# Reordering the second chunk's attention work on ScalarE, VectorE and TensorE in a fused mLSTM and GELU kernel

## The chip, the cores and the metric

The kernel runs on one core of a Trainium2 chip. The metric is the time of one execution on the device in microseconds (us); several runs are taken and their median is compared. The engines are called as the profile has them: PE is TensorE (PEld its weight loads), DVE is VectorE, ACT is ScalarE, POOL is GpSimd, SP is SyncE, which issues most DMA transfers. Each engine works through its own instructions in order and waits on semaphores for the others.

## What is computed

The reference has two parts. The first is an mLSTM cell over q, k, v of shape (4 batches, 8 heads, 768 steps, 40 dimensions), with gates i, f and o:

```
m_new  = max(f + m, i)
f_stab = exp(f + m - m_new);  i_stab = exp(i - m_new)
C = f_stab * C + i_stab * outer(v, k);   n = f_stab * n + i_stab * k
y = sigmoid(o) * (C @ q) / max(|n . q|, 1)
```

The second takes the 3072 rows of y as x (3072 x 320) and computes `g = h * sigmoid(1.702 h)` with `h = x @ w_in` (320 x 2048), and then `g @ w_out` (2048 x 320).

## The kernel before

The 768 steps are cut into six chunks of 128 (w = 0 to 5). Inside a chunk the cell is computed in matrix form: scores of keys against queries times a matrix of decay weights, then products with v; from chunk to chunk a state (40 x 41 for each of 32 head pairs, two heads above each other on the partitions) is carried. From w = 1 on a chunk is worked in two halves of 64 steps, with `state_mid` between them. Work is further cut into two groups of 16 heads, c = 0 and 1.

The main loop goes over the chunks. For each w TensorE first does the up products of that chunk (x times w_in, `up` for w = 0, `up_fast` from w = 1 on), and then the down products (`down` or `down_fast`) in small blocks. Between the blocks of chunk w the attention work of chunk w + 1 is interleaved: `attention(w)` returns a dictionary from a block's number to the calls that are made right after that block. So for w = 0 there are 16 blocks of `down` (L835, eight recorded matmuls of 128x320 each), in the order batch 0, 1, 2, 3 with two blocks each for the first half of w_out, then the same for the second half; among them stands the attention work of the second chunk, w = 1. That stage runs from 65.9 to 108.6 us in the profile, and the change lies in it.

The order of every engine's instructions is that of the program text (a manual schedule); semaphores follow from what each instruction reads and writes. The names that matter, with their lines in the kernel before:

- `fill_squares(q_sq)` (L119, ACT): two copies that complete the square layout of the queries, which two DMA transfers have brought. `block_transposes` (L415, DVE) then turns them into qT, four times 128x512.
- `columns` (L387, L391, ACT): exponentials of per-step factors, kept in `cols`.
- `weights_exp(1, c)` (L463, ACT): 16 exponentials of 128x64. `weights_mask(1, c)` (L470, POOL): two masks over 64 partitions each.
- `scale` (L619, POOL) makes vw, `decay` (L610) multiplies a state by its decay factor; on POOL for state_mid, on DVE inside `carry`.
- `carry(1, c)`: products of keys and vw on TensorE (L633), and additions of the result to the decayed states on DVE (L642). The decay of the second half (L610 on DVE) stands between the two additions.
- `convert(n)`: one piece (128x512) of the expert weights, from 64-bit words to floats: two ACT instructions (L254, L258, `convert_begin`) and four DVE instructions (L270, L275, L281, L282, `convert_end`). Pieces 17, 18 and 19 are the last ones of w_out.
- `weight_sums` (L847, POOL): differences of quarters of w_out, kept in t_sb. `keep_w01` (L914, issued on POOL): a copy of one quarter to DRAM.
- `scores(1, c)`: products on TensorE (L490) and a multiplication with the masked weights on DVE (L493). `values(1, c)`: products with v (L534) and with the states (L542), then DVE forms y: L548 and L549 add them, L500 to L509 divide and gate.
- PSUM holds eight banks: four are taken by the four open sums of `down`, and two pairs (`banks`) go round among carry, scores and values: scores take the pairs that carry wrote, the values of a group take both pairs, one for L534 and one for L542.
- `seam_out`, `seam_in`, `seam_turn`: y goes to DRAM and back in square blocks (for c = 0 issued on SP, for c = 1 on ACT; the way back on SP), and DVE turns it (L603). `split_x` (ACT, L765) and `split_on` (DVE, L773 and on) cut x into a high and a low part for the up products of chunk 1.
- `split_high`, `split_rest` (ACT), `split_diff`, `split_low`, `split_rest_low` (DVE): the same for w_in.

The calls of `attention(1)` are listed in `calls`, and `at` gives for each entry the block behind which it is made. Before the change scores stand behind block 6 (counted from 0), the two values behind 8 and 9.

Of the kernel before, what the change touches and what calls it, by code (L numbers as in the profile page):

```python
# [14 lines left out]
OP = mybir.AluOpType  # L15
# [17 lines left out]
def kernel(  # L33
# [81 lines left out]
    def fill_squares(t):  # L115

        x = t[:, 32:].rearrange("r (m d) -> r m d", d=D)
        for i in (0, 64):
            A.copy(out=x[i + 32:i + 64, :, 0:D - 32], in_=x[i:i + 32, :, 32:D])  # L119
# [124 lines left out]
    def convert(n):  # L244
        convert_begin(n)
        convert_end(n)

    def convert_begin(n):
        convert_high(n)
        convert_low(n)  # L250
# [9 lines left out]
    def convert_end(n):  # L260
        convert_mid(n)
        convert_add(n)
# [116 lines left out]
    def columns(w):  # L379
        if w == 0:  # L380
            pt = banks("p_cols")[:, 0, :]
            T.transpose(pt[:, 0:3 * BH], stacked[w], full)
            c = cols[w] = gate.tile([L, 4 * BH], FP, bufs=1, name="cols")
            A.activation(out=c[:, 2 * BH:3 * BH], in_=pt[:, 2 * BH:3 * BH], func=AF.Exp, scale=-1.0)
            return
        c = cols[w]
        A.activation(out=c[:, BH:3 * BH], in_=c[:, BH:3 * BH], func=AF.Exp, scale=-1.0)  # L387
        d = raw[w][:, 3 * BH:].rearrange("p (j i x) -> p i x j", i=2, x=2)
        for i in range(2):
            r = slice(i * 64, i * 64 + 64)  # L390
            A.activation(out=c[r, 3 * BH:].rearrange("p (x j) -> p x j", x=2), in_=d[r, i], func=AF.Exp)  # L391
# [233 lines left out]
    def carry(w, c):  # L625
        js = slice(c * NJ, (c + 1) * NJ)
        pc = banks("p_c")
        n = 2 if 0 < w < NW - 1 else 1
        for j in range(NJ):
            for i in range(2):  # L630
                for x in range(n):
                    t = slot(i, x) if w else slice(0, L)
                    T.matmul(pc[i * 64:i * 64 + D, x, j * D1:(j + 1) * D1], k_cols(w, t, c * PH + 2 * j + i),  # L633
                             vw[w, c][t, 2 * j + i, :], start=True, stop=True)
        new = lambda x: pc[:, x, 0:NJ * D1].rearrange("r (j d) -> r j d", d=D1)
        if w == 0:
            A.copy(out=state[1][:, js], in_=new(0))
            return
        for x, dst in enumerate((state_mid, state[1 - w % 2])[:n]):
            if x:  # L640
                decay(w, c, x, V)
            V.tensor_tensor(out=dst[:, js], in0=new(x), in1=dst[:, js], op=OP.add)  # L642


    def up(w, j, between, first=None):

# [72 lines left out]
    def split_diff(n):  # L719
        V.scalar_tensor_tensor(out=w_diff[1, n], in0=w_high[n], scalar=-1.0 - 1.0 / BASE, in1=w_in[n], op0=OP.mult,  # L720
                               op1=OP.add)

    def split_low(n, engine):
        if n < 2:
            w_low[n] = win.tile([128, 2, 512], FR, tag="wa" if n else "wb", name="w_low")
        engine.tensor_tensor(out=w_low[n] if n < 2 else w_low[1, n], in0=w_in[n], in1=w_high[n], op=OP.subtract)
# [17 lines left out]
    def split_rest_low():  # L744
        wr = w_rest[0]
        V.tensor_tensor(out=wr[64:128, 0::2], in0=w_in_x[0:64], in1=wr[0:64, 0::2], op=OP.subtract)
        V.tensor_tensor(out=wr[64:128, 1::2], in0=w_in_x[64:128], in1=wr[64:128, 1::2], op=OP.subtract)
# [164 lines left out]
    def keep_w01():  # L912
        w01_row.append(rows.tile([128, NH, DH], FP, tag="w01", bufs=1, name="w01_row"))
        G.dma_start(out=w01_row[0], in_=w01)  # L914
# [112 lines left out]
    fetched = {0: range(10, 13), 1: range(13, 18), 3: (18, 19)}  # L1027

    def attention(w):
        at = (0, 1, 3, 3, 5, 6, 8, 8, 9, 11, 12, 13) if w == 1 else (0, 0, 1, 3, 2, 4, 5, 6, 6, 10, 11, 11)  # L1030
        calls = [[(columns, w)][w == 1:] + [(scale, w, 0), (scale, w, 1), (decay, w, 0, 0), (decay, w, 1, 0)],
                 [(weights_mask if w == 1 else weights, w, 0)], [(weights, w, 1)], [(carry, w, 0), (carry, w, 1)], [(open_gates, w)],
                 [(scores, w, 0), (scores, w, 1)], [(values, w, 0)], [(seam_out, w, 0), (seam_in, w, 0)],
                 [(values, w, 1), (seam_out, w, 1), (seam_in, w, 1)], [(seam_turn, w, 0), (split_x, w, 0)], [(seam_turn, w, 1), (split_x, w, 1)], [(split_on, w)]]
        if w == 1:
            calls[2:4] = [], calls[3] + [(weight_sums, 0)] + calls[2]
        side = {}
        for i, c in zip(at, calls):
            side.setdefault(i, []).extend(c)
        return side  # L1040

    for w in range(NW):
# [119 lines left out]
        for i, block in enumerate(blocks):  # L1162
            if w == 0 and i == 0:
                columns(1)
                convert_begin(17)
                weights_exp(1, 0)
                fill_squares(q_sq)
                convert_end(17)
                for n in (1, 3, 5, 7):
                    block_transposes(1, n)  # L1170
            if w == 0 and i in (4, 5):
                convert(14 + i)
            if w + 2 < NW and i == (6 if w == 0 else 0):
                load_gates(w + 2)
            if w == 0 and i == 13:
                load_squares(w + 2, "k")
            if w == 0 and i == 15:
                load_squares(w + 2, "q")
            block()
            run(side.get(i, []))  # L1180
            if w == 1 and i == 4:
                last_sums(1, 0, (2, 3))
            if w == 0 and i == 5:
                keep_w01()
                wait_for(w_out_flat[1][:, 4 * 512:])
                weight_sums(1)
                weight_sums(3)
            if w == 0 and i == 5:
                split_high(0)
                split_rest()  # L1190
                split_high(1)
            if w == 0 and i == 9:
                split_diff(0)
                split_low(0, V)
                split_rest_low()
            if w and more:
                if i == 11:
                    fetch_diff(w + 1, (0, 1))
                    fetch_low(w + 1)
                    if w + 2 < NW:  # L1200
                        load_squares(w + 2, "k")
                if w + 2 == NW and i == 8:
                    room_out(0, 8, 8, "k_sq", 2592)
                    out_part(0, 8)
                    out_part(0, 12)
                if i == 13:
                    fetch_diff(w + 1, (2, 3))
                    if w + 2 == NW:
                        fetch_w01()
                    if w + 2 < NW:  # L1210
                        load_squares(w + 2, "q")
# [30 lines left out]
```

## Time and profile before

| | us |
|---|---|
| median of 3 runs | 443.29 |
| lowest and highest | 443.14, 443.64 |
| the profiled execution | 444.92 |
| its span, first to last instruction | 443.2 |
| stage with the change, first down product to first fast up product | 65.9 to 108.6 |
| TensorE busy over the span | 438.0 |
| VectorE, ScalarE, GpSimd busy | 349.5, 246.2, 130.4 |

The granted TensorE clock of the run was 1.0. The chain of waits is followed back from the last instruction: at each step to what released it, or to the instruction before it on the same engine. In a timeline a row gives the start and the duration in us, the engine, the line, the operation, what it writes and reads with shapes, and, in brackets, how long the engine was idle before it and what ended that. "x4" means that four like instructions are merged into one row.

### The profile page before, as it was taken

How to read it: one execution, taken by the hardware profiler on the slowest of the kernel's cores; microseconds unless marked ns; L12 is line 12 of the kernel's file. 1: busy time of each engine (PE TensorE's matmuls, PEld its weight loads, DVE VectorE, ACT ScalarE, POOL GpSimd, SP SyncE). 2: the span in 40 equal slices, each digit the busy share in tenths (PEclk: the TensorE clock that was granted, in tenths of full speed). 3: DMA queues.
4: the chain of work that ended last, by engine and by line, in shares of the span. 5: the costliest groups of instructions: out<-in, count | busy, mean ns of one | idle time of the engine just before them, and what ended most of it. 6: DMA issues, size and time to landing. Idle time of an engine off the chain costs nothing.

```text
span 443.2 us, 12203 instructions
## 1 busy us (share of the span) xinstructions
PE 438.0 (99%) x4967; PEld 382.1 (86%) x4967; DVE 349.5 (79%) x701; ACT 246.2 (56%) x536; POOL 130.4 (29%) x133
## 2 busy tenths in 40 slices
PE   8999999999999999999999999999999999999996
PEld 6877887777889999888999888999888999988996
DVE  4898998989999876779686778686769656988990
ACT  5676779902887701687701486900386912397720
POOL 6411337540066700135700044710035620022100
PEclk9999999999999999999999999999999999999999
DMA  8999999227779327979226997305999305810000
GB/s 168 195 291 224 239 246 186 61 47 191 179 204 175 48 66 218 236 101 190 34 54 167 288 112 164 58 19 139 308 154 159 61 19 137 276 61 0 3 29 30
DMA packets 130008, 61.37 MB, mean 138 GB/s; under 512 B 102128, under 2 KB 122592, under 8 KB 129952
## 3 DMA queue, kind: packets, MB, share of 16 engines
q1 hardware_dynamic: 120512, 54.86, 57.7%
q10 hardware_dynamic: 8768, 4.28, 3.3%
q0 software_dynamic: 672, 1.46, 1.3%
q8 instruction: 39, 0.64, 0.7%
q14 instruction: 17, 0.14, 0.1%
HBM read 49.76 MB, written 10.81 MB: 137 GB/s over the span
## 4 chain that ended last, share of the span: by engine, by line
PE 97%; DVE 1%; DMA 1%; issue 0%; ACT 0%; SPq 0%; DVEq 0%
PE p_out L888 28%; PE p L806 17%; PE p_h L806 17%; PE p_out L835 8%; PE p_h L657 7%; PE p L963 6%; PE p L534 2%; PE p L490 2%; PE p L542 2%; PE p L633 2%; PE p_h L666 2%; PE p L406 2%; PE p_s L479 1%; PE p_o L524 1%; DMA k_sq<-in_k_dram 1%; DVE state L610 0%
## 5 line engine op out<-in xcount | busy, mean ns | idle before, releaser
L856 POOL TENSOR_TENSOR g<-g 128x512 f32<-128x512 f32 x16 | 20.6, 1298 | 119.4 <-ACT g L784 119.4
L888 PE MATMUL p_out<-w_out,g 128*128 128x160 f32 x384 | 55.2, 300 | 0.0
L888 PEld LDWEIGHTS p_out<-w_out,g 128*128 128x128 f32 x384 | 53.1, 190 | 0.5
L765 ACT ACTIVATE x_high<-xT 128x512 fp32r<-128x512 f32 x10 | 6.3, 632 | 76.9 <-DVE xT L603 76.9
L784 ACT ACTIVATE g<-g 128x512 f32<-128x512 f32 x80 | 46.4, 628 | 2.9 <-DVE g L825 2.7
L823 ACT ACTIVATE g<-p 128x512 f32<-128x512 f32 x40 | 21.8, 597 | 34.9 <-PE p L806 33.5
L825 DVE SCALAR_TENSOR_TENSOR g<-p,g 128x512 f32<-128x512 f32 x40 | 25.7, 684 | 18.5 <-ACT g L823 10.5
L463 ACT ACTIVATE wt<-wt,cols 128x64 f32<-128x64 f32 x160 | 39.0, 341 | 0.1
L888 PE MATMUL p_out<-t_sb,s 128*128 128x160 f32 x256 | 37.8, 301 | 0.0
L893 DVE TENSOR_TENSOR o_sb<-o_sb,p_out 128x160 f32<-128x160 f32 x56 | 16.8, 319 | 26.4 <-PE p_out L888 26.2
L888 PEld LDWEIGHTS p_out<-t_sb,s 128*128 128x128 f32 x256 | 35.5, 190 | 0.2
L835 PE MATMUL p_out<-w_out,g 128*128 128x320 f32 x128 | 35.7, 436 | 0.0
L835 PEld LDWEIGHTS p_out<-w_out,g 128*128 128x128 f32 x128 | 23.9, 190 | 9.6
L825 DVE SCALAR_TENSOR_TENSOR g<-p_h,g 128x512 f32<-128x512 f32 x40 | 25.9, 680 | 5.6 <-PE p_h L806 5.0
L657 PE MATMUL p_h<-xT,w_in 128*128 128x256 f32 x128 | 29.8, 385 | 0.1
L657 PEld LDWEIGHTS p_h<-xT,w_in 128*128 128x128 f32 x128 | 23.6, 190 | 5.4 <-issue 2.2
L823 ACT ACTIVATE g<-p_h 128x512 f32<-128x512 f32 x40 | 23.3, 597 | 7.9 <-PE p_h L806 7.9
L470 POOL TENSOR_SCALAR_AFFINE_SELECT wt<-wt 64x1024 f32<-64x1024 f32 x20 | 24.3, 1217 | 7.1 <-ACT wt L463 6.2
L806 PE MATMUL p_h<-x_diff,w_diff 128*128 128x512 f32 x80 | 25.1, 394 | 0.0
L806 PE MATMUL p<-x_rest,w_rest 128*128 128x512 f32 x80 | 25.1, 395 | 0.0
L806 PE MATMUL p_h<-x_rest,w_rest 128*128 128x512 f32 x80 | 25.0, 394 | 0.0
L806 PE MATMUL p<-x_diff,w_diff 128*128 128x512 f32 x80 | 25.0, 393 | 0.0
(224 smaller groups left out, 1051.6 us busy)
## 6 DMA issues: line engine op xcount, KB each, us to landing
w_diff<-w_row SPq DMA_DIRECT2D x16, 512.0 KB, 5.7
wt<-m_row SPq DMA_DIRECT2D x20, 256.0 KB, 5.3
bits<-in_moe_w_in_dram SPq DMA_DIRECT2D x8, 512.0 KB, 8.4
out_dram<-o_sb SPq DMA_DIRECT2D x24, 160.0 KB, 3.0
q_sq<-in_q_dram SPq DMA_DIRECT2D x10, 320.0 KB, 9.1
eo<-in_o_gate_dram SPq DMA_DIRECT2D x5, 640.0 KB, 6.6
bits<-in_moe_w_out_dram SPq DMA_DIRECT2D x8, 320.0 KB, 5.6
q_sq<-x_row SPq DMA_DIRECT2D x10, 256.0 KB, 2.7
```

What stands on the lines that cost most here:

```text
L463: A.activation(out=x[:, h, :], in_=x[:, h, :], func=AF.Exp, scale=-1.0, bias=cols[w][:, c * PH + h:c * PH + h + 1])
L470: G.affine_select(out=r, in_=r, compare_op=OP.is_ge, fill=0.0, base=0, pattern=[[0, PH], [1, HL]], channel_multiplier=-1)
L657: T.matmul(ph[j][i][:, t], w_in[f // 4][:, c, f % 4 * 128:f % 4 * 128 + 128], x[:, c, t], start=(first and c == 0 and n == 0), stop=(not f ...
L784: A.activation(out=g, in_=g, func=AF.Gelu_apprx_sigmoid)
L806: T.matmul(dst[i], a(i), x, start=(first and m == which[0]), stop=(last and m == which[-1]))
L823: A.activation(out=g[:, i, :], in_=side[i], func=AF.Copy, scale=-BASE)
L825: V.scalar_tensor_tensor(out=g[:, i, :], in0=main[i], scalar=1.0 + 1.0 / BASE, in1=g[:, i, :], op0=OP.mult, op1=OP.add)
L835: T.matmul(po, gs[w, f // 2][:, f % 2, b * L:(b + 1) * L], w_out_sb[f // NH][:, f % NH, :], start=(f == 0), stop=(f == NF - 1))
L856: G.tensor_tensor(out=a10, in0=a00, in1=a10, op=OP.subtract)
L888: T.matmul(po, a(f), b[:, f, :], start=(f == 0), stop=(f == NH - 1))
L893: V.tensor_tensor(out=dst, in0=x, in1=po, op=OP.add)
L963: T.matmul(dst, g_part[n, b, f // 2][:, f % 2], wo[n, f][0][:, wo[n, f][1]], start=(f == order[0] and n < 2), stop=(f == order[-1] and n > 0))
```

## The change

In the second chunk's attention work:

- `fill_squares(q_sq)` comes directly after `columns(1)`, ahead of the conversion of piece 17 and of the first exponentials; the transposes stand on VectorE ahead of the second half of that conversion.
- Pieces 18 and 19 are converted right after `carry`, ahead of the second group's exponentials, and no longer behind blocks 4 and 5. `keep_w01` is issued behind `weight_sums(0)`, ahead of the second group's masks.
- `carry(1, c)` no longer decays state_mid for the second half's state on VectorE: ScalarE copies the new part alone into `state[0]`. After `values(1, 1)`, ScalarE multiplies state_mid by the decay into `state[1]` (`late_states`, 16 instructions), and VectorE adds the two (`late_sums`).
- The gates' tanh moves from behind block 5 to behind block 3, scores from 6 to 5, values from 8 and 9 to 6 and 7, the second turning of x and `split_on` from 12 and 13 to 13; the splits of w_in that stood behind block 9 now follow the second values.

```
         if w == 0:
             A.copy(out=state[1][:, js], in_=new(0))
             return
+        if w == 1:
+            V.tensor_tensor(out=state_mid[:, js], in0=new(0), in1=state_mid[:, js], op=OP.add)
+            A.copy(out=state[0][:, js], in_=new(1))
+            return
...
+    def late_states(w):
+
+        d = cols[w][:, 3 * BH + BH // 2:4 * BH]
+        for j in range(BH // 2):
+            A.activation(out=state[1][:, j, :], in_=state_mid[:, j, :], func=AF.Copy, scale=d[:, j:j + 1])
+
+    def late_sums():
+        V.tensor_tensor(out=state[0], in0=state[0], in1=state[1], op=OP.add)
...
-        at = (0, 1, 3, 3, 5, 6, 8, 8, 9, 11, 12, 13) if w == 1 else (0, 0, 1, 3, 2, 4, 5, 6, 6, 10, 11, 11)
+        at = (0, 1, 3, 3, 3, 5, 6, 6, 7, 11, 13, 13) if w == 1 else (0, 0, 1, 3, 2, 4, 5, 6, 6, 10, 11, 11)
...
         if w == 1:
-            calls[2:4] = [], calls[3] + [(weight_sums, 0)] + calls[2]
+            calls[2:4] = [], calls[3] + [(convert, 18), (convert, 19), (weight_sums, 0), (keep_w01,)] + calls[2]
+            calls[8].insert(1, (late_states, w))
+            calls[8] += [(split_diff, 0), (split_low, 0, V), (split_rest_low,), (late_sums,)]
...
             if w == 0 and i == 0:
                 columns(1)
+                fill_squares(q_sq)
                 convert_begin(17)
                 weights_exp(1, 0)
-                fill_squares(q_sq)
-                convert_end(17)
                 for n in (1, 3, 5, 7):
                     block_transposes(1, n)
-            if w == 0 and i in (4, 5):
-                convert(14 + i)
+                convert_end(17)
...
             if w == 0 and i == 5:
-                keep_w01()
                 wait_for(w_out_flat[1][:, 4 * 512:])
                 weight_sums(1)
                 weight_sums(3)
...
-            if w == 0 and i == 9:
-                split_diff(0)
-                split_low(0, V)
-                split_rest_low()
```

## The prediction

> **What bounds the kernel now.** I read the page first, then the chain of waits in the stage that the change touches, then the timelines of VectorE, GpSimd and ScalarE there. Times in us are counted from the start of the span.
>
> ```profile
> PE 438.0 (99%) x4967; PEld 382.1 (86%) x4967; DVE 349.5 (79%) x701; ACT 246.2 (56%) x536; POOL 130.4 (29%) x133
> ...
> PE 97%; DVE 1%; DMA 1%; issue 0%; ACT 0%; SPq 0%; DVEq 0%
> ```
>
> TensorE is busy 438.0 of 443.2 us and is 97% of the chain: what comes early gains nothing unless a TensorE wait ends, and what makes TensorE wait is paid in full. The chain in the changed stage:
>
> ```profile
> 75.97 6.66 PE p_out L835 x24
> 82.62 2.02 PE p L490 x128
> 84.65 4.50 PE p_out L835 x16
> 89.15 1.07 PE p L534 x64
> 90.23 0.93 PE p L542 x64
> ```
>
> No piece of another engine stands in this chain from 65.9 to 108.6: block products (L835), carry (L633, before these lines), scores (L490) and values (L534, L542) find their inputs ready. All the stage can give back is at its end, where the next piece, the first up product, takes 3.81 against 3.67 for its like: 0.14.
>
> VectorE, GpSimd and ScalarE before that (start, us, what):
>
> ```profile
> 69.78 0.74 DVE L270 TENSOR_SCALAR w_out<-w_out 128x512 f32<-128x512 f32 x1 [0.69 <-ACT w_out L254]
> 70.56 1.39 DVE L275 TENSOR_SCALAR w_out<-w_out 128x512 uint32<-128x512 uint32 x1
> 71.88 1.27 DVE L281 TENSOR_SCALAR t_sb<-t_sb 128x512 uint16<-128x512 uint16 x1
> 73.18 1.02 DVE L282 CUSTOM_DVE_ANT_0 w_out<-t_sb,w_out 128x1024 uint16<-128x1024 uint16 x1
> 75.47 3.99 DVE L415 STREAM_TRANSPOSE qT<-q_sq 128x512 f32<-128x512 f32 x4 [1.27 <-ACT q_sq L119]
> ...
> 79.82 1.20 DVE L610 TENSOR_TENSOR state<-state_mid,cols 128x328 f32<-128x328 f32 x1
> ...
> 82.95 0.42 DVE L270 TENSOR_SCALAR w_out<-w_out 128x512 f32<-128x512 f32 x1
> 83.40 0.43 DVE L275 TENSOR_SCALAR w_out<-w_out 128x512 uint32<-128x512 uint32 x1
> 83.74 0.75 DVE L281 TENSOR_SCALAR bits<-bits 128x512 uint16<-128x512 uint16 x1
> 84.53 0.69 DVE L282 CUSTOM_DVE_ANT_0 w_out<-bits,w_out 128x1024 uint16<-128x1024 uint16 x1
> ```
>
> ```profile
> 74.23 2.35 POOL L470 TENSOR_SCALAR_AFFINE_SELECT wt<-wt 64x1024 f32<-64x1024 f32 x2 [0.58 <-ACT wt L463]
> 76.66 2.92 POOL L847 TENSOR_TENSOR t_sb<-w_out 128x1280 f32<-128x1280 f32 x1
> 79.54 2.50 POOL L470 TENSOR_SCALAR_AFFINE_SELECT wt<-wt 64x1024 f32<-64x1024 f32 x2
> 81.98 0.89 POOL L914 DMA_DIRECT2D w_row<-w_out  x1
> ```
>
> ```profile
> 70.21 3.94 ACT L463 ACTIVATE wt<-wt,cols 128x64 f32<-128x64 f32 x16
> ```
>
> The four instructions of a conversion (L270, L275, L281, L282) take 0.74, 1.39, 1.27 and 1.02 while GpSimd computes (vw and state_mid, 68.7 to 73.65), and 0.42, 0.43, 0.75 and 0.69 from 82.95 on, when GpSimd computes nothing until 87.5. Between 69.8 and 74.2 each slow VectorE instruction ends 0.3 to 0.6 after a GpSimd instruction ended, and the next GpSimd instruction ends late in turn: one VectorE instruction, one GpSimd instruction, alternately. The decay (L610) does the same, 1.20 beside a mask. Transposes (L415) and operations that read PSUM (the score multiplication L493, two in 2.35 from 87.32) keep their duration beside GpSimd. So conversions 18 and 19 (82.95 to 87.4) now stand in a hole of GpSimd's work; where they land after the change decides the time.
>
> **The change, part by part.**
>
> *Fill and transposes first.* The fill (1.26, from the row at L119) follows the columns, which end at 69.05. Its second half needs the squares' second transfer, landed at 69.90, so it ends at 70.6 instead of 75.4; conversion 17's ScalarE half (1.1) ends at 71.7, and the first 16 exponentials (3.94) at 75.6, not 74.15. The four transposes run from 70.65 to 74.5. Conversion 17's VectorE half (four instructions, 2.3 alone) follows; its last meets the first mask half (1.15) and ends about 77.65.
>
> *Carry.* VectorE loses two decays and two adds (1.20+0.50+0.50+0.50 = 2.7) and keeps two adds of 0.5: 77.6 to 78.6. ScalarE gains two copies of 128x328 from PSUM (nearest row: L839, 128x320, 0.43) and ends them at 76.5. Both hide: scores are the next to need these banks.
>
> *Conversions 18 and 19, ahead of the second exponentials.* ScalarE: four at 0.57, 76.4 to 78.7; the exponentials then run from 78.7 to 82.65, not 75.46 to 79.4. GpSimd has the first masks until 78.75, weight_sums(0) (2.92), the issue of keep_w01 (0.89), then the second masks, which can't start before 82.7. On VectorE I let the engines alternate as from 69.8 to 74.2. Conversion 18's first instruction gets in at 78.75, ends 79.05; weight_sums(0) holds until 81.95; the second instruction to 82.25, the third to 82.95; mask half to 84.05; the fourth to 84.6; mask half to 85.7; conversion 19's first to 86.0, its rest (0.43, 0.74, 0.69) to 87.85. So the conversions end 0.45 later than now (87.4), with everything that needs them two block products earlier on TensorE.
>
> *Scores and values.* The order of kinds on TensorE stays, so do its 0.2 us joints. Scores start at 75.90+4.50 = 80.40 (transposes end 74.5, banks are free at 78.6: no wait) and end at 82.42; one block product, 2.35, to 84.77. values(1,0) needs the first score multiplication (L493, 1.2), which VectorE reaches at 87.8: wait until 89.05. Its second half (L542) writes the bank that the second multiplication still reads until 90.2, then takes 1.05: end 91.25. Unhindered it would end at 84.77+2.01 = 86.78. **The stall is 4.47 us.** Bounds: if the engines did not hold each other up, VectorE would go from 74.5 through three conversions of 2.28 and the adds (1.0) to 82.4, and the second multiplication, behind a mask ending at 85.0, would end at 86.25: stall 0.5. If a further mask half (1.15) falls between two instructions of the conversion: 5.6. I take 4.47, since the rows of 69.8 to 74.2 are the same four instructions, some 8 us earlier.
>
> *values(1,1)* comes one block later, at 93.65; its banks are free when the sums L548 and L549 (0.84 each, behind 91.35) end at 93.1. The margin was 0.5 before (92.95 against 93.44) and stays. Eight block products follow instead of six.
>
> *keep_w01 and the gates' tanh* move ahead: 0.89 on GpSimd, which it does beside VectorE's third instruction (at 81.98 the issue kept its 0.89 beside an unstretched L610), and 1.25 on ScalarE (behind the exponentials; the weight splits after it have until 108). Its 640 KB move while the DMA engines are nearly idle; the next to write w01 does so at 125. The rows of y go out on SP ahead of any store, as now.
>
> *late_states*: 16 ScalarE instructions of 128x41 at about 0.24 (L463, 128x64) = 3.8, behind values(1,1), 95.7 to 99.6. Behind them on ScalarE stand the two seam_out issues of the second half, whose y is made by 100.1: cover. Bound from above: at 0.43 each (the 128x320 copy) 6.9, ending 102.6, 2.5 late. *late_sums* is one VectorE add of 128x656, 0.84 (L549) to 1.22 (L726), behind 4.9 of weight splits, at 105. Then the second rows turn at about 109; x_high is ready near 109.7 and TensorE wants it at 113.0. The cover is 3.2, which also holds for the second split_x, now queued on ScalarE behind the eviction of the third output, whose buffer waits for the first output's store on SP, itself behind seam_in. So the 0.14 at the start of the up products goes.
>
> **Sum**: +4.47 - 0.14 = +4.3. The profiled execution took 444.92 (443.2 of span and 1.7 around) and would take 449.2; the median of the runs shown, 443.29, is 1.6 below it, so I forecast 447.6.
>
> **Rivals.**
> *A: the engines do not hold each other up here.* Stall 0.5, less 0.14: 443.7. Against it: the stretched rows above, and L610 at 79.82.
> *B: not slower.* VectorE is relieved by 2.7 and x is ready 3 us ahead. If GpSimd reached weight_sums(0) only behind the conversions, the first multiplication would end before 84.8 and the second before 85.8, the points from which it decides. Then there is no stall, the 0.14 goes, and of the 0.55 that the next such stage loses (39.16 against 38.61 for the last one; the chain shows VectorE L610 and L642 ahead of its scores) up to all: 442.6. Against it: weight_sums(0) needs only w_out's first half, long converted, and stands directly behind the first masks.
> *C: TensorE runs slowly after its wait.* At the start the chip shows it: the 512-column product of L446 takes 0.63 when it starts at 6.09 and 0.39 at 11.24, and follows at 0.43 and 0.22. A slow stretch as long as from 6.09 to 11.24 at half speed would add 2.6: 450.2. Against it: TensorE had barely worked by then, while here it idles once, for 4.3. [...] No row of this trace has such a wait in mid-kernel.
> *D: the second rows of x come too late* (late_states dear and everything behind it): it needs over 3.2, and the upper bound is 2.5.
>
> **How the numbers follow.** Forecast 0.62, C 0.16, A 0.11, B 0.08, D and others 0.03. The time is that of the likeliest, 447.6; its own range is 446.5 to 448.7 (the further mask half upward, one fewer downward). The range of 8 in 10 runs from A's 443.7 to C's 450.2. Within 0.2% (0.89 us, about what a measurement of this kernel tells from no change) lie A and most of B: same 0.13; faster 0.05; slower 0.82.
>
> **What would show it.** Right: TensorE idle about 4 us ahead of L534, near 85 to 89, released by VectorE L493, with L493 starting near 87.8 and not 85; conversions 18 and 19 stretched to several us between 78 and 88; a chain with VectorE and GpSimd pieces there; the first up product 3.67. Transposes near 70.65 and exponentials ending at 75.6 and 82.65 test the rest. Wrong: L493 before 84.8, or conversion rows at 0.42 and 0.43 beside weight_sums(0). Block products slower than 0.27 behind the wait would be C.

## The result, and the profile after

The changed kernel takes 454.3 us (median of six runs, 453.59 to 455.79) where the kernel before took 443.97 (443.14 to 444.36): a ratio of 1.024 with an interval of 1.0216 to 1.0263. It is slower by 10.3 us. The forecast was 447.6 with a range up to 450.2, so the sign was right and the size was not. The profiled execution took 454.94 us with a span of 453.2, against 444.92 and 443.2 before: 10.0 us more.

From the page of the kernel after: busy times, the granted clock in 40 slices, and the chain's shares.

```profile
PE 441.2 (97%) x4967; PEld 384.3 (85%) x4967; DVE 347.8 (77%) x698; ACT 250.2 (55%) x554; POOL 129.9 (29%) x133
...
PEclk9999999979999999999999999999999999999999
...
PE 13%; DMA 2%; DVE 0%; ACT 0%; ACTq 0%; SPq 0%; issue 0%; DVEq 0%
```

TensorE is busy 3.2 us longer although it has the same 4967 matmuls, and one slice of the clock row shows 7. The chain covers only 15% of the span, because, followed back, it ends in the last chunk at DMA transfers of x (the last one issued at 384.57) and goes no further. It says nothing about the changed stage any more, so that stage has to be read from timelines.

TensorE in the changed stage of the kernel after (start, duration, engine, line, operation; in brackets the idle time before and what ended it):

```profile
82.45 2.42 PE L848 MATMUL p_out<-w_out,g 128*128 128x320 f32 x8
89.43 2.00 PE L534 MATMUL p<-v_st,wt 64*64 64x41 f32 x62 [4.57 <-DVE wt L493]
...
93.12 3.81 PE L848 MATMUL p_out<-w_out,g 128*128 128x320 f32 x8
```

The same stage in stretches of 5 us: busy time and number of instructions for PE, PEld, DVE, ACT and POOL, then the granted clock, the DMA share and GB/s.

```profile
80.00:85.00 5.00, 4.87 (x138) 3.39 (x136) 4.26 (x4) 5.00 (x17) 3.65 (x2) 1.00 0.17 48
85.00:90.00 5.00, 0.57 (x20) 0.57 (x22) 4.93 (x7) 4.98 (x9) 3.62 (x4) 0.91 0.32 88
90.00:95.00 5.00, 5.00 (x123) 4.33 (x120) 2.19 (x3) 4.16 (x11) 4.92 (x2) 0.50 0.01 3
95.00:100.00 5.00, 5.00 (x138) 3.77 (x137) 3.30 (x8) 1.75 (x8) 0.36 (x1) 0.90 0.30 60
100.00:105.00 5.00, 5.00 (x20) 3.53 (x19) 4.86 (x9) 0.12 (x1) 0.00 (x0) 1.00 0.47 125
```

TensorE waits for the first score multiplication (L493), and then the granted clock is one half from 89.1 to 95.9, for 6.83 us. The block product that takes 2.35 elsewhere in the stage takes 3.74 here (its row of 3.81 less the overlap with the next).

Set against the kernel before, piece by piece on TensorE, the 10.0 us are made up like this:

| place | predicted | measured |
|---|---|---|
| stall at values(1, 0) (forecast: 4.28 ahead of it and 0.19 inside; measured: all ahead) | +4.47 | +4.63 |
| values(1, 0) at half clock, 3.69 against 2.01 | 0 | +1.68 |
| the next block product, 3.74 against 2.35 | 0 | +1.39 |
| joints, the short gaps between one kind of product and the next, up to the first fast up product (115.95 against 108.46, 7.49 late) | 0 | -0.21 |
| first up product, 3.93 against 3.82 | -0.14 | +0.12 |
| seventh up product, at 139.32 | 0 | +1.05 |
| first up product of the last chunk | 0 | +1.46 |
| all else | 0 | -0.14 |
| sum | +4.3 | +9.98 |

The term of the last chunk is run-to-run: a transfer of x (issued 384.57) takes 5.4 us to land, 2.3 before; here GpSimd's fetch of weights was issued ahead of it (384.20), before it came behind it. A second profile of the same kernel (c_after, below) has no such step, e4_copy_first has one of 1.4. The other terms are what the experiments are about.

VectorE, GpSimd and ScalarE of the kernel after, in the order of the engines:

```profile
77.29 1.50 DVE L282 CUSTOM_DVE_ANT_0 w_out<-t_sb,w_out 128x1024 uint16<-128x1024 uint16 x1
78.71 0.89 DVE L640 TENSOR_TENSOR state_mid<-p,state_mid 128x328 f32<-128x328 f32 x2
80.67 2.42 DVE L270 TENSOR_SCALAR w_out<-w_out 128x512 f32<-128x512 f32 x1 [1.07 <-ACT w_out L254]
83.13 0.76 DVE L275 TENSOR_SCALAR w_out<-w_out 128x512 uint32<-128x512 uint32 x1
...
86.75 1.49 DVE L282 CUSTOM_DVE_ANT_0 w_out<-bits,w_out 128x1024 uint16<-128x1024 uint16 x1
88.17 2.34 DVE L493 TENSOR_TENSOR wt<-p,wt 128x1024 f32<-128x1024 f32 x2
```

```profile
77.05 2.74 POOL L470 TENSOR_SCALAR_AFFINE_SELECT wt<-wt 64x1024 f32<-64x1024 f32 x2 [4.14 <-ACT wt L463]
79.88 2.94 POOL L860 TENSOR_TENSOR t_sb<-w_out 128x1280 f32<-128x1280 f32 x1
...
86.24 3.01 POOL L470 TENSOR_SCALAR_AFFINE_SELECT wt<-wt 64x1024 f32<-64x1024 f32 x2 [2.60 <-ACT wt L463]
```

```profile
71.26 0.61 ACT L119 COPY q_sq<-q_sq 32x512 f32<-32x512 f32 x1 [1.57 <-DMA q_sq<-in_q_dram]
...
79.23 0.84 ACT L641 COPY state<-p 128x328 f32<-128x328 f32 x2 [2.25 <-DVE state_mid L640]
...
82.26 3.91 ACT L463 ACTIVATE wt<-wt,cols 128x64 f32<-128x64 f32 x16
```

Three things are to be seen. The first instruction of conversion 18 (80.67) takes 2.42 where it takes 0.42 alone: it ends 0.28 after weight_sums(0) (79.88 to 82.82) ended. The fill waits for the squares' second transfer, landed at 71.23, so everything behind it starts from there. And ScalarE, done with the first exponentials at 76.98, stands for 2.25 us with its copy of the new state: it waits for VectorE's addition (L640), which has the transposes and conversion 17 ahead of it. The later landing and this wait put the second exponentials at 82.26 instead of the forecast 78.7. With the fill first and the states behind, the chain is serial: landing, fill, transposes, conversion 17, additions (VectorE), copies and conversions' first half (ScalarE), second exponentials, second masks (GpSimd), second multiplication.

### The profile page after: what moved, and what is told of

Its sections match the earlier page's. It is cut to its first block, busy times and chain, and to the rows that moved or that the text cites. A ratio compares the mean times of both kernels' runs of the same rounds, so it can differ in the third digit from the quotient of the medians.

```text
span 453.2 us, 12216 instructions
## 1 busy us (share of the span) xinstructions
PE 441.2 (97%) x4967; PEld 384.3 (85%) x4967; DVE 347.8 (77%) x698; ACT 250.2 (55%) x554; POOL 129.9 (29%) x133
## 3 DMA queue, kind: packets, MB, share of 16 engines
q10 hardware_dynamic: 8768, 4.28, 3.3%
q0 software_dynamic: 672, 1.46, 1.2%
## 5 line engine op out<-in xcount | busy, mean ns | idle before, releaser
L848 PE MATMUL p_out<-w_out,g 128*128 128x320 f32 x128 | 37.1, 448 | 0.0
L819 PE MATMUL p<-x_high,w_high 128*128 128x512 f32 x80 | 24.6, 399 | 1.2 <-ACT x_high L778 1.2
```

Of the source, the lines that this page charges most:

```text
L819: T.matmul(dst[i], a(i), x, start=(first and m == which[0]), stop=(last and m == which[-1]))
L848: T.matmul(po, gs[w, f // 2][:, f % 2, b * L:(b + 1) * L], w_out_sb[f // NH][:, f % NH, :], start=(f == 0), stop=(f == NF - 1))
```

## The experiments

Line numbers are those of each kernel's own text. "The wait" is TensorE's ahead of values(1, 0), "the lag" how much later than in the kernel before's profile the first fast up product starts (7.49 after). It includes a difference that arises ahead of the stage: the stage's first block product starts at 65.77 before and 65.78 after, but between 64.35 (e7_fill_first) and 66.81 (e5_states) in the others. The idle time in brackets counts from the modelled end of the matmul ahead; waits in the text count from where the next piece starts when nothing holds it, which is 0.05 to 0.2 more. The kernel before was measured anew beside three groups of runs, at 444.84 (e1 to e4), 445.15 (e6 to e9) and 444.3 us (c_after, e8b, e5, e10).

### What the wait itself costs, and what the clock

The first two were to separate the wait from the slow clock behind it: one fills the wait with products that write unused columns of an open bank, the other moves scores and values back to their old places, behind blocks 6, 8 and 9.

```diff
+    def filler(n):
+        for _ in range(n):
+            T.matmul(o_ps[0, 3][:, 384:512], gs[0, 0][:, 0, 0:128], w_out_sb[0][:, 0, 0:128], start=False, stop=False)
...
+            calls[6].insert(0, (filler, 18))
```

> The changed kernel with 18 products of 128x128 put on TensorE ahead of the first values, into 128 unused columns of an open output bank (about 0.21 us each, 3.9 us in all, the result is not read). They lie inside the 4.6 us in which TensorE waits for the score multiplications. Theory 1 (the long wait halves TensorE's clock, which costs 1.68 us in the values and 1.39 us in the block product behind them): the clock stays at 1.0, the first values take 2.0 us again, the whole time falls by 3.1 us to about 451.2. Rival 2 (the slow values come from something else, such as the banks or the weights being read while other engines use them): values stay at 3.7 us and the time at about 454.3.

Measured: 462.58 (459.33 to 466.67), the kernel before beside it 444.84, ratio 1.0363 (1.0286 to 1.0439). The time doesn't tell the theories apart. In the profiled execution, the longest of the four, the squares' transfers were issued at 65.4 and landed at 77.98, 6.7 later than after, TensorE waited 6.88 ahead of the scores already, and the clock dropped there for 10.24 us; the filler stood behind that in series (4.1 us). In two later chunks TensorE lost another 4.2 and 3.0 ahead of the first up product. Only its tail is of use: the filler's own end is followed by values(1, 0) in 2.00 and a block product in 2.35 at full clock.

```diff
-        at = (0, 1, 3, 3, 3, 5, 6, 6, 7, 11, 13, 13) if w == 1 else ...
+        at = (0, 1, 3, 3, 5, 6, 8, 8, 9, 11, 12, 13) if w == 1 else ...
```

> The changed kernel with the places of the kernel before: scores behind 7 block products, values behind 9 and 10, tanh of the gates and the second turning where they were. All else stays changed. Theory 1 (the conversions and masks end at the same time, about 90.5, and TensorE merely came too early): the first values wait 0.3 to 0.6 us, the clock stays at 1.0, about 444.5. Rival 2 (the moved conversions, the copies and the late states cost by themselves): 447 or more.

Measured: 448.31 (447.34 to 451.19), ratio 1.0081 (1.0052 to 1.011), which is in the range of the second expectation (447 or more). TensorE of this kernel, and its stretch behind the wait:

```profile
90.35 1.24 PE L534 MATMUL p<-v_st,wt 64*64 64x41 f32 x64 [1.29 <-DVE wt L493]
```

```profile
89.00:92.50 3.50, 2.21 (x129) 2.14 (x128) 2.43 (x3) 3.42 (x5) 3.44 (x3) 1.00 0.02 5
92.50:96.00 3.50, 3.50 (x17) 2.27 (x9) 3.24 (x3) 0.87 (x1) 3.42 (x2) 0.51 0.00 0
```

The later places cut the wait to 1.36, not to the expected 0.3 to 0.6: the squares landed at 72.15, and the second multiplication ended at 91.43, both 0.92 later than after. The clock still halves, for 3.41 us, and one block product takes 4.00. The lag is 3.35, and no step follows it. So the attention work is too late even for the old places, and here the slow clock followed a wait of 1.36. Where a run of this kernel showed a mean clock of 1.0, it took 447.34 and 447.82, still 2.5 and 3.0 above the kernel before; at 0.996, 448.24 to 449.33, and at 0.992, 451.19. A mean of 0.996 over 447 us is one stretch of 3.5 us at half speed, so the wait alone and the wait with one slow stretch differ here by about 1 us.

The same with eight filler products ahead of values(1, 0):

> The kernel with the later places (scores behind 7, values behind 9 and 10 block products, all else changed), with 8 products of 128x128 on TensorE (about 1.7 us) ahead of the first values, into unused columns of an open output bank. There the first values waited 1.36 us in the profile and the clock went to 0.5 for 3.41 us, with the block product behind at 4.00 instead of 2.35 us. Theory 1 (a wait of 1.4 us next to the small products of the values is enough to halve the clock): clock 1.0 in that stretch, block product 2.35, time about 1.7 us below that kernel's 448.3, 446.6. Rival 2 (the slow block product isn't due to the wait): product still near 4.0, time 448.3 or more.

Measured: 453.02 (450.26 to 457.11), the kernel before beside it 445.15, ratio 1.0151 (1.0079 to 1.0223). Inconclusive as e1_fill was: in the profiled execution, the longest of the four, the transfers were issued at 66.1 and landed at 75.71, TensorE waited 2.39 ahead of the scores, and the clock dropped there for 3.41. Behind the filler there was neither wait nor slow clock:

```profile
92.27 1.95 PE L860 MATMUL p_out<-w_out,g 128*128 128x128 f32 x16
94.14 1.14 PE L534 MATMUL p<-v_st,wt 64*64 64x41 f32 x64
```

Both fillers show what late squares do, and in both profiles the values behind uninterrupted products ran at a granted clock of 1.00. Whether a filled wait saves anything wasn't shown: two runs of this kernel had a mean clock of 1.0 and still took 450.26 and 450.68, more than the 448.31 without the filler. In these two profiles SyncE's issues of weight pieces ahead of the squares took 7.1 and 8.3 us instead of 5.0; why stays open.

### Which work makes the multiplications late

```diff
-            calls[2:4] = [], calls[3] + [(convert, 18), (convert, 19), (weight_sums, 0), (keep_w01,)] + calls[2]
+            calls[2:4] = [], calls[3] + [(convert, 18), (convert, 19)] + calls[2] + [(weight_sums, 0), (keep_w01,)]
```

> The changed kernel with weight_sums(0) and keep_w01 behind the second group's masks on GpSimd, so that GpSimd computes nothing beside conversions 18 and 19. Theory 1 (the two engines take turns): the first instruction of conversion 18 takes 0.42 instead of 2.42 us, the conversions end near 85.2, the first multiplication near 86.4; the second still waits for the masks (exponentials end at 86.2, masks at 88.6) and ends near 89.8. [...] Rival 2 (VectorE does not wait for GpSimd): first instruction unchanged, 454.3.

Measured: 454.39, ratio 1.0209 (1.017 to 1.0247): as slow as after. VectorE of this kernel:

```profile
83.09 0.43 DVE L270 TENSOR_SCALAR w_out<-w_out 128x512 f32<-128x512 f32 x1 [1.10 <-ACT w_out L254]
...
91.04 1.22 DVE L493 TENSOR_TENSOR wt<-p,wt 128x1024 f32<-128x1024 f32 x1 [2.36 <-POOL wt L470]
```

Without the sums beside it the instruction of 2.42 takes 0.43, so the stretching is GpSimd's doing. The conversions end at 87.5, 13.9 behind the landing (73.65) instead of 17.0, and the first multiplication follows at once; but the second now waits 2.36 for the second masks and ends 18.6 behind the landing, against 19.3. So the sums beside the conversions cost 0.7 of the end. TensorE waits three times (1.20 ahead of the scores, 2.19 and 2.34 at the values), none of them over 2.4, and the clock still halves for 6.83. So the slow clock doesn't need one wait as long as after's 4.63.

```diff
-            V.tensor_tensor(out=state_mid[:, js], in0=new(0), in1=state_mid[:, js], op=OP.add)
             A.copy(out=state[0][:, js], in_=new(1))
+            V.tensor_tensor(out=state_mid[:, js], in0=new(0), in1=state_mid[:, js], op=OP.add)
```

> The changed kernel with ScalarE's copy of the second half's state traced ahead of VectorE's addition in the carry. Theory 1 (the copies waited 2.25 us only because they were traced behind VectorE's additions on the same bank): the copies start at about 77.0 and conversion 18's first half at about 77.8, 2.2 us earlier; the second masks then begin near 84 and take turns with conversions 18 and 19, so that the multiplications gain less than that or nothing, between 452.3 and 455. Rival 2 (ScalarE's queue alone set the end): everything 2.2 us earlier, wait of 2.4 us, clock at 1.0, about 449.

Measured: 455.52, ratio 1.0223 (1.0172 to 1.0274), 0.5 above the first expectation's range. ScalarE, then VectorE:

```profile
77.10 0.74 ACT L640 COPY state<-p 128x328 f32<-128x328 f32 x2
```

```profile
80.33 3.02 DVE L275 TENSOR_SCALAR w_out<-w_out 128x512 uint32<-128x512 uint32 x1
...
84.67 1.36 DVE L270 TENSOR_SCALAR w_out<-w_out 128x512 f32<-128x512 f32 x1
86.06 1.25 DVE L275 TENSOR_SCALAR w_out<-w_out 128x512 uint32<-128x512 uint32 x1
...
88.60 2.35 DVE L493 TENSOR_TENSOR wt<-p,wt 128x1024 f32<-128x1024 f32 x2
```

The copies no longer wait, the second exponentials end at 83.96 and not 86.17. But conversion 18 now meets weight_sums(0) with its second instruction (3.02, where after its first took 2.42), the earlier masks fall beside conversion 19 (1.36 and 1.25), and the second multiplication ends at 90.94, no earlier. What ScalarE's queue gave, the alternation of VectorE and GpSimd took back.

```diff
                 columns(1)
-                fill_squares(q_sq)
                 convert_begin(17)
                 weights_exp(1, 0)
+                fill_squares(q_sq)
+                convert_end(17)
                 for n in (1, 3, 5, 7):
                     block_transposes(1, n)
-                convert_end(17)
```

> The changed kernel with the order of the kernel before at the stage's start: conversion 17 and the first exponentials, then the fill, then the transposes. All else stays changed. In five profiles with the fill first the second score multiplication ended 18.6 to 19.5 us after the squares' second transfer landed (71.2 to 78.0). Theory 1 (the landing sets the end because ScalarE's whole queue stands behind the fill): the first exponentials start near 70.2 whatever the landing, and the multiplications' end no longer moves with it. But ScalarE's copies still stand behind VectorE's additions, which now come after the transposes (80.3), so that the second exponentials end near 87, the masks near 89.3 and the second multiplication near 90.5, as in a run with an early landing: 452.5 to 454.5. Rival 2 (the early fill is the whole loss): below 449.

Measured: 453.12 (451.62 to 454.64), ratio 1.0171 (1.0118 to 1.0225). Its steps came out where they were expected: first exponentials at 70.33, ScalarE's copies at 79.90 after a wait of 4.37 for the addition, second exponentials ending at 86.99, second multiplication ending at 90.67. That is as early as after (90.51), although the squares landed 1.9 later here (73.13): the fill now hangs on the end of the exponentials (74.25) and not on the landing. In the eight profiles that keep after's head of the stage and its sums, the second multiplication ends 19.2 to 19.5 behind the landing, whenever that is. So the early fill ties the whole chain to a transfer and gains nothing for it, and without it the loss is still most of what it was.

The fill alone, put first in the kernel before:

```diff
                 columns(1)
+                fill_squares(q_sq)
                 convert_begin(17)
                 weights_exp(1, 0)
-                fill_squares(q_sq)
-                convert_end(17)
                 for n in (1, 3, 5, 7):
                     block_transposes(1, n)
+                convert_end(17)
```

> The kernel before with only the first edit: fill ahead of conversion 17 and of the first exponentials, transposes ahead of the second half of conversion 17. Conversions 18 and 19, carry, scores and values stay where they were. Theory 1: with a landing near 71 the multiplications end near 89, in time for values behind 9 and 10 block products: 444 to 445.5; with a landing of 73 or later they end later by as much and TensorE waits, 447 or more, clock below 1.0. Rival 2 (the early fill costs whatever the landing): 449 or more in every run.

Measured: 447.29 (446.32 to 450.34, ten runs), ratio 1.006 (1.0034 to 1.0086). I had expected no more than 445.5 with squares as early as these (landed 70.83): a miss. They were early only on the clock of the span. The stage itself began at 64.35 in this execution, so they landed 6.5 behind its start, against 5.5 after and 4.1 before. VectorE, TensorE, and the stretch behind TensorE's wait:

```profile
80.70 2.16 DVE L610 TENSOR_TENSOR state<-state_mid,cols 128x328 f32<-128x328 f32 x1
82.90 0.50 DVE L642 TENSOR_TENSOR state<-p,state 128x328 f32<-128x328 f32 x1
```

```profile
83.45 1.16 PE L490 MATMUL p<-qT,kT 40*64 40x64 f32 x64 [1.15 <-DVE state L642]
```

```profile
84.70:88.10 3.40, 3.40 (x7) 2.23 (x8) 3.33 (x6) 3.32 (x5) 1.82 (x2) 0.50 0.31 85
```

It wasn't the multiplications that came late but the carry's additions, which now stand behind conversion 17 and whose banks the scores need; a decay between them took 2.16 beside weight_sums(0) (0.50 before). The wait between the two halves of the scores is only 1.37, and again 3.41 us at half clock follow it; the lag is 2.18, and 3.6 counted from the start of the stage.

### The states alone

The kernel before with nothing but the states edit: `late_states` behind values(1, 1), `late_sums` behind the splits of w_in. Two versions, which differ in the order of two lines of `carry`:

```diff
+        if w == 1:
+            V.tensor_tensor(out=state_mid[:, js], in0=new(0), in1=state_mid[:, js], op=OP.add)
+            A.copy(out=state[0][:, js], in_=new(1))
+            return
```

> The kernel before with only the states' edit: in the carry VectorE adds and ScalarE copies behind it, late states on ScalarE and the late sum on VectorE. Fill, conversions, scores and values as before. Theory 1 (a copy traced behind VectorE's addition on the same bank waits for it): the transposes end at 79.5, the additions near 80.3, ScalarE's second exponentials end near 84.6 instead of 79.4, conversions 18 and 19 near 90.4, the multiplications near 91.5 and 92.7; values behind 9 blocks wait 2.4 us and the clock drops: 447.5 to 450. Rival 2 (taking 2.7 us from VectorE makes the multiplications earlier): no slower than before, within 0.5 us.

```diff
+        if w == 1:
+            A.copy(out=state[0][:, js], in_=new(1))
+            V.tensor_tensor(out=state_mid[:, js], in0=new(0), in1=state_mid[:, js], op=OP.add)
+            return
```

> The same as the states' edit alone, but with ScalarE's copy traced ahead of VectorE's addition. Theory 1: the copies start at 75.5 behind the fill, the second exponentials end near 80.2, conversions 18 and 19 near 86, the multiplications near 87.2 and 88.4, 1.3 us earlier than before; no wait at the values, clock 1.0, and the time equals that of the kernel before within 0.5 us, perhaps 0.1 to 0.4 below it, with 1.3 us more room for a late transfer. Rival 2 (the late states on ScalarE delay the way of y or the up products): 1 us or more above the kernel before.

Measured, beside the kernel before at 444.3: 450.44 (449.55 to 452.5), ratio 1.0138 (1.0106 to 1.0171), for the addition first, 0.4 above its expected range; 445.06 (443.78 to 447.53, twelve runs), ratio 1.0008 (0.9983 to 1.0033), for the copy first. With the addition first, ScalarE, VectorE and TensorE:

```profile
80.79 0.84 ACT L641 COPY state<-p 128x328 f32<-128x328 f32 x2 [4.35 <-DVE state_mid L640]
81.65 3.93 ACT L463 ACTIVATE wt<-wt,cols 128x64 f32<-128x64 f32 x16
```

```profile
91.82 2.35 DVE L493 TENSOR_TENSOR wt<-p,wt 128x1024 f32<-128x1024 f32 x2
```

```profile
93.10 1.60 PE L534 MATMUL p<-v_st,wt 64*64 64x41 f32 x61 [2.90 <-DVE wt L493]
```

With the copy first:

```profile
74.32 1.01 ACT L640 COPY state<-p 128x328 f32<-128x328 f32 x2
75.36 3.93 ACT L463 ACTIVATE wt<-wt,cols 128x64 f32<-128x64 f32 x16
```

```profile
85.57 2.34 DVE L493 TENSOR_TENSOR wt<-p,wt 128x1024 f32<-128x1024 f32 x2
```

```profile
87.97 1.14 PE L534 MATMUL p<-v_st,wt 64*64 64x41 f32 x64
```

ScalarE's copy and VectorE's addition read the two halves of one PSUM tile (`pair`, 128 x 2 x 512: two different banks, although two of the expectations say the same bank) and write different things. Still the one that comes second in the program text waits for the one that comes first. The wait is a semaphore in the compiled program: in e5_states the copy waits for VectorE's, in e10_states_copy the addition for ScalarE's. What it costs with the addition first is 4.35 us of ScalarE's queue, with the exponentials, the masks and the conversions behind it, a wait of 2.90 on TensorE and 6.83 us at half clock. The swap of two lines is worth 5.4 us. With the copy first the states edit is neither faster nor slower than the kernel before; the earlier multiplications (the second ends 23.25 behind the start of the stage instead of 23.90) gain nothing, since TensorE had no wait there to lose.

That also says what the whole change could have given. Values behind block 6 and 7 need the two multiplications by 84.8 and 85.8, which is 19.0 and 20.0 behind the start of the stage. Even in this kernel, where the second ends earliest of all, they end 22.1 and 23.25 behind it. No version measured beats the kernel before.

### The step at the seventh up product

ScalarE's queue of the kernel after, ACTq being its DMA issues, and TensorE:

```profile
135.36 0.37 ACTq L743 DMA_DIRECT2D w_row<-w_diff  x1
135.82 1.05 ACT L747 CAST w_low<-w_low 128x1024 fp32r<-128x1024 f32 x1 [3.74 <-DVE kT L415]
```

```profile
139.32 0.73 PE L819 MATMUL p<-x_rest,w_rest 128*128 128x512 f32 x2 [0.91 <-ACT g L836]
```

ScalarE stands 3.74 us ahead of the cast. The profile names VectorE, but what stands first in its queue is the DMA issue of 135.36. It keeps a split row of w_diff in DRAM. In the compiled program it signals its end on the same semaphore as the keep of another row issued at 128.91, which landed at 135.28, and waits for it. Before, and in e2_later, e5_states, e7_fill_first, e9_later_fill and e10_states_copy, its semaphore belonged to an older transfer, and there is no step. All six profiles in which ScalarE issues it with the shared semaphore have one, of 1.1 to 1.6. To take it away, GpSimd issues that one transfer:

```diff
-        nc.scalar.dma_start(out=row[n], in_=x.rearrange("p c m -> p (c m)").bitcast(FP))
+        (G if row is w_diff_row and n == 3 else nc.scalar).dma_start(out=row[n], in_=x.rearrange("p c m -> p (c m)").bitcast(FP))
```

> The changed kernel with one transfer, the keeping of the last w_diff row during the next chunk's up products, issued by GpSimd and not by ScalarE. In the changed kernel ScalarE's queue stood at that issue from 131.3 to 135.4, until the transfer that used the same completion semaphore before it had landed (135.28), and TensorE then waited about 1.05 us for ScalarE. Theory: the wait goes and the time falls by 1.0 to 1.2 us, to about 453.2. Rival: the wait comes from transfers being slow at that point; then it stays, about 454.3.

Measured: 454.8, the kernel before beside it 445.15, ratio 1.0212 (1.0168 to 1.0256), not the expected 453.2. The step is gone, the lag is the same on both sides of it (10.1), but the stage began 0.95 later, the squares landed at 72.91, and the lag was larger from the start. So the same kernel was run again beside the changed kernel itself:

> The changed kernel again, unaltered, as a control beside the next three. Theory: about 2.4% above the kernel before, 9 to 11 us, as at first; with a later landing of the squares' second transfer than 71.2 correspondingly more. The second score multiplication ends 18.6 to 19.5 us after that landing.

> The changed kernel with the keeping of the last w_diff row issued by GpSimd instead of ScalarE, again, beside the unaltered one. In the first look at it the wait of about 1.05 us in the next chunk's up products was gone, but the landing was later (72.9) and no unaltered run stood beside it. Theory: 1.0 to 1.6 us below the unaltered changed kernel of the same call, for equal landings, and no step in TensorE's lag between its first and its last up product. Rival: no difference in time beyond that of the landings.

Measured: 454.2 (451.52 to 455.12) for the changed kernel, 453.18 (451.83 to 455.11) with the issue moved, the kernel before 444.3; ratios 1.022 (1.0184 to 1.0256) and 1.021 (1.0176 to 1.0244). ScalarE with the issue moved:

```profile
133.19 1.05 ACT L747 CAST w_low<-w_low 128x1024 fp32r<-128x1024 f32 x1 [0.48 <-DVE w_low L739]
```

The cast waits 0.48 and not 3.74, and the lag stays at 8.21 across the place where the changed kernel's goes from 8.86 to 10.37. The traces show the wait gone; in the times about 1 us of it can't be told from runs that scatter over 3.5.

## Why the prediction was wrong, step by step

*Rival C, "TensorE runs slowly after its wait"*, is the step that failed. It had a chance of 0.16 and a price of 2.6, with the doubt that TensorE "idles once, for 4.3". Every profile in which TensorE waited over 1.3 us in this stage shows the half clock (granted 0.50, for 3.41 to 10.24 us), the changed kernel's in both profiles, and the price was 3.07. The prediction took it as a special case, and it belonged in the sum: 447.6 would have been 450.7. Between the profiled executions, 449.2 forecast and 454.94 measured, it is the largest part of the 5.7 that are missing; the seventh up product has 1.05 and the last chunk 1.46 of the rest. The mean clock of after's six runs, 0.984 to 0.992, works out to 7 to 14.5 us at half speed in each of them (453 times the missing share, times two). The products at the start from which the 2.6 was worked out had a granted clock of 1.00 beside them (before, 6 to 12 us), so they were no half clock of this kind; no run shows what slowed them.

*"The stall is 4.47 us"*: 4.63, but by errors that cancel. *Fill and transposes first*: "ends at 70.6" took the landing of before, 69.90; it landed at 71.23, and the fill ended at 71.87, the transposes at 75.89. *Carry*, "ends them at 76.5. Both hide": the copies started at 79.23, since they waited for VectorE's additions. I had costed them by their duration and the banks' next user, and not asked what the copy itself waits for: this wait of 2.25, and 1.3 from the later landing, put the second exponentials 3.5 late (86.17 instead of 82.65). *Conversions 18 and 19*: with the masks that late, fewer GpSimd instructions fell between VectorE's, and the last conversion ended at 88.25, 0.4 behind the forecast 87.85. The rows agree with that alternation: 2.42, 1.49 and 1.50 beside GpSimd's instructions, the 2.42 ending 0.28 after GpSimd's sums, and 0.42 to 0.73 from 83.81 to 86.07, when it computed nothing. e3_sums_behind and e4_copy_first show both sides of it.

*"So the 0.14 at the start of the up products goes"*: it didn't; the first up product took 3.93.

*The rest of the kernel at nothing*: the step at the seventh up product, 1.05, was in no part of the sum and in no rival. The change adds no DMA issue on ScalarE, and moves none of those; but the order of all engines' issues in the program text is another one, and this transfer signals on another semaphore than before (109 instead of 102). Which of the moves does that wasn't tested. The 1.46 of the last chunk was not foreseen either; it comes and goes between runs.

*Rivals A, B and D* are out: the engines do hold each other up, the multiplications ended 4.6 and 4.7 behind the points from which B decides, and x was ready in time. In that part the forecast held: `late_states` took 1.85 for eight, 0.23 each (0.24 forecast), and was done at 100.1, ahead of the rows of y at 103.1; keep_w01 kept its 0.89 and the tanh its 1.25. The slow stretches were 3.41, 6.83 or 10.24 long. They don't follow one length of wait: TensorE of the kernel after was idle for the whole 3.41 us ahead of its slow stretch (85.71 to 89.13), but in e2_later and e7_fill_first it had waited 1.36 and 1.37.

## What to carry to other kernels

Where TensorE has run without a gap, price a new wait at its length and at least one slow stretch behind it (the shortest here, 3.41 us at half clock, followed waits of 1.36 and 1.37), and don't leave the second to a rival. Before an instruction that reads PSUM is put on another engine, ask what stands ahead of it in the text on the same tile, and what that waits for: two lines in the wrong order cost 5.4 us in the states edit alone, which in the other order changed nothing. And moving work earlier can pay only where something waits for it; here nothing did, and the time by which it had to be ready moved forward with it.

## What the runs showed of the hardware

- TensorE's granted clock stood at 0.50 in this stage (75 to 105 us) for 3.41 us (e2_later, e7_fill_first, e9_later_fill), 6.83 (after, e3_sums_behind, e5_states, e6_fill_back) or 10.24 (c_after, e1_fill, e4_copy_first, e8_ring, e8b_ring), which is one, two and three times the same, and not at all in before and e10_states_copy. Idle time alone doesn't tell when. Three stretches of this length in a row of e9_later_fill, then two of e1_fill (columns as above):

```profile
79.58:82.99 3.41, 2.17 (x9) 1.18 (x7) 3.34 (x5) 1.85 (x8) 1.42 (x2) 1.00 0.16 31
82.99:86.41 3.42, 2.27 (x129) 2.21 (x130) 2.33 (x4) 2.76 (x6) 3.34 (x2) 1.00 0.02 5
86.41:89.82 3.41, 3.41 (x7) 2.05 (x7) 3.34 (x5) 3.41 (x15) 1.65 (x2) 0.50 0.36 100
```

```profile
86.33:89.74 3.41, 3.36 (x124) 3.36 (x128) 2.39 (x1) 3.41 (x9) 3.33 (x3) 0.50 0.02 5
89.75:93.16 3.41, 3.41 (x19) 2.31 (x15) 3.31 (x7) 3.41 (x14) 0.82 (x2) 0.50 0.67 185
```

  The first stretch, block products and 1.24 us idle, was followed by the full clock; the second, the small products of the scores (40x64) and 1.15 idle, by the half clock. In e1_fill a stretch at half clock filled with scores for 3.36 of 3.41 us was followed by another at half clock, and that one, nearly all block products, by the full clock (from 93.16). In e2_later and e7_fill_first, 1.25 and 1.15 idle beside small products had the half clock behind them; in e3_sums_behind, 1.48 idle beside block products had the full clock. That the kind of product decides is my reading of these stretches; neither it nor a limit was measured.
- Where VectorE and GpSimd worked side by side, their instructions ended in turn (before, 69.8 to 74.2; after, 79.88 to 83.1). An instruction of 0.42 took up to 2.42 (L270 of after, at 80.67, beside weight_sums(0)), one of 0.43 up to 3.02 (L275 of e4_copy_first, at 80.33), and the last of a conversion (L282) went from 0.69 to 1.49 (after, at 86.75, beside the second masks). The transposes (four in 3.99 beside masks and sums in before; all 20 that write qT in that kernel took 1.08 to 1.16 each) and the multiplications that read PSUM (two in 2.34 beside masks and sums in after, all ten of that kernel 1.21 to 1.23 each) kept their length.
- A DMA issue on ScalarE's queue of after stood until 135.36, just behind the landing (135.28) of an unrelated transfer that used its semaphore before, and the arithmetic behind it stood with it (3.74 us ahead of the cast; 0.48 with the issue on GpSimd).
